# Reordering the start of a transformer block's forward and backward kernel, with two deviations by ScalarE's root and some stores on another queue

## The chip, the cores and the metric

One core of one Trainium2 chip runs the whole kernel as one program. The metric is the device time of one execution in microseconds (us); several executions are timed and the median is given. The engines are PE (TensorE; PEld is its weight load), DVE (VectorE), ACT (ScalarE), POOL (GpSimd) and SP (SyncE, which here only issues transfers). SP, ACT and POOL can each issue DMAs into a queue of their own. Every engine executes its own list of instructions in order, and waits for other engines through semaphores.

## The reference

A pre-LN transformer block, forward and then the gradients of all inputs and weights, in bfloat16, for 2048 rows of width 512, 32 heads of 16, a hidden width of 1792 and a window of 8 positions with a stride of 2:

```python
qkv = (layernorm(x) @ wqkv)            # 32 heads of 16
idx = pos[:, None] - arange(8) * 2     # each row looks at 8 earlier rows
logits = einsum("bhsd,bhswd->bhsw", q, k[idx]) * 16 ** -0.5   # -1e9 where idx < 0
h  = x + einsum("bhsw,bhswd->bhsd", softmax(logits), v[idx]) @ wo
h2 = h + gelu(layernorm(h) @ w1 + b1) @ w2 + b2
# outputs: h2, and by jax.vjp of h2 with grad_out:
# gradients of x, wqkv, wo, w1, b1, w2, b2
```

The outputs that the text below names are out_1, the gradient of x ("gx"), and out_2, the gradient of wqkv (its pieces are "wgsq").

## The kernel before, in words

The 2048 rows are worked in four chunks (0 to 3) of 512 rows, each of four tiles of 128. For each chunk the forward attention comes first (norm, projections k, q, v, products, softmax, output projection), then the feed-forward part, then the backward pass; the weight gradients and the gradient of x of the last chunk end the program.

**How the order is set.** The functions of the kernel do not issue instructions; they record operations in a `Plan` (lines 62 to 145), each with its engine, its estimated cost, and what it reads and writes. `emit` (L118) then issues them in the order of a long table of numbers, `ORDER` (from L1283), and a second table, `HOMES` (from L1367), gives every buffer its place in SBUF or its bank in PSUM. So on each engine the operations stand in a fixed list, and an operation whose input is late holds up all that stand behind it on that engine. Two tensors that have the same PSUM banks in HOMES follow each other: the later one is written only when the earlier has been read out. On SP, eight semaphores are used in rotation for its DMAs, so the ninth transfer waits for the first to land.

**The names around the change.** `load` (L267) fetches inputs and `store` (L271) writes results, both on SP unless told otherwise. `evict` (L280) copies a PSUM tensor to SBUF on ACT (L283). The first norm (`layernorm`, L338) of chunk 0 goes tile by tile: tiles 1 and 3 (`STA`) get their sums on ACT (L348 to L351), tiles 0 and 2 on DVE (L368, L369), then a root on ACT (L375), a reciprocal (L378) and the scaling (L395) on DVE. PE transposes the result (L434) and three copies on ACT and one on DVE put it into `ln1T` of chunk 0.

For chunks 1 to 3 the four tiles are done together: sums on DVE (L368 and L369, four times), variance plus epsilon on DVE (`ve`, L380), the power -1/2 on POOL (L383), mean times the reciprocal deviation on DVE (L386), then four scalings on ACT (L391, x as input and `ln1_1` for chunk 1 as output). The transposed `ln1T` of these chunks comes by a DMA transpose on SP (L277).

`p1_proj` (L648) makes k and q for the chunk with `ln1T`: 16 matmuls on PE each (L658), in two halves of two PSUM banks, and evicts each half into `kt0` or `qt0` on ACT. `p1_v` (L668) makes v (L683, evicted to `tmv`). `dots` (L502) forms the products of q with the shifted k on DVE (`prf`, L506) and sums them over a head on PE (L514). `p1_attn` (L714) does the softmax: mask (L720), maximum (L723), its subtraction by a matmul with minus the identity (`nident`, made on ACT in L320; L728), exponent on ACT (L731). ACT keeps one table of functions at a time; L310 and L312 are one-column roots and exponents that bring a table in early. The second half of the forward pass starts with L810; the feed-forward work needs `ln2T`.

At the end, `ln_bwd` (L582) takes the input gradient of the norm from PSUM (matmuls of `p3_gl1`, L1030): ACT scales and sums (L588, L590), DVE sums the product with the norm's output (L591), ACT forms `u` (L594), and DVE adds (L600, L601) to give `gx`, of which `p3_gl1` stores four pieces of a chunk (L1038). Each piece reads all four tiles. The last matmuls are groups of `wg_group` (L1042) that sum the gradient of wqkv (L1056); each group is cast on ACT (L283) and stored from SP (L273). The setting `GXP` (L1269) lists which pieces of `gx` are stored by POOL's queue.

Of the kernel before, what the change touches and what calls it, by code (L numbers as in the profile page):

```python
# [13 lines left out]
ACT = mybir.ActivationFunctionType  # L14
ALU = mybir.AluOpType
# [6 lines left out]
EPS = 1e-5  # L22
# [126 lines left out]
def kernel(  # L149
# [21 lines left out]
    V, A, T, G, SY = nc.vector, nc.scalar, nc.tensor, nc.gpsimd, nc.sync  # L171
# [4 lines left out]
    S, D = xf.shape  # L176
# [8 lines left out]
    scale = DH ** -0.5  # L185
# [14 lines left out]
    mhalf = cst("mhalf", [P, TPC], F32)  # L200
# [70 lines left out]
    def store(dst, ap, src, src_ap, kb, key=None, skey=None, q="SP", tag="store", row=1):  # L271
        e, us = (SY, 0.45) if q == "SP" else (G, 0.6)
# [65 lines left out]
    def layernorm(c, src, MV, ST, VE, NM, R, mv, st, ve, nm, rs, dst, eng, tag, per=TPC):  # L338
        sk = lambda j: None if tag == "1" and c in PM else j
        for g0 in range(0, TPC, per):  # L340
# [38 lines left out]
            else:  # L379
                op("DVE", 0.08, lambda s=s, sq=sq: V.tensor_scalar(out=ve[:, s], in0=mv[:, s, 1], scalar1=1.0 / D if sq else EPS, scalar2=EPS if sq else None, op0=ALU.mult if sq else ALU.add,  # L380
                                                                   **({"op1": ALU.add} if sq else {})),
                   r=[(MV, t) for t in ts], w=[(VE, k)], tag="ve" + tag)
                op("POOL", 1.1, lambda s=s: G.tensor_tensor(out=rs[:, s], in0=ve[:, s], in1=mhalf[:, 0:per], op=ALU.pow), r=[(VE, k), MHALF],  # L383
                   w=[(R, t) for t in ts], tag="pow" + tag)
# [620 lines left out]
    def p3_gl1(c):  # L1005
# [31 lines left out]
        for j, ap in enumerate(perm_rows(gxf[c * CH:(c + 1) * CH, :])):  # L1037
            store(None, lambda ap=ap: ap, gx, lambda j=j: gx()[32 * j:32 * j + 32], 128, q="POOL" if (c, j) in GXP else "SP", tag="gxst")  # L1038

# [128 lines left out]
    for i in range(0 if W2PE else 4):  # L1168
        r = F // 4
# [93 lines left out]
STA = (1, 3)  # L1263
WQA = ()
# [4 lines left out]
GXP = ((2, 0), (2, 1), (2, 2), (2, 3), (3, 0), (3, 1), (3, 2), (3, 3))  # L1269
# [165 lines left out]
```

## Time and profile before

| what | value |
|---|---|
| median of 3 runs | 548.23 us (546.52 to 549.38) |
| the profiled execution | 548.3 us |
| its span | 546.4 us |
| mean granted clock of PE | 0.99 |
| PE busy | 529.8 us (97%) |
| DVE busy | 467.9 us (86%) |
| ACT busy | 337.8 us (62%) |
| POOL busy | 17.5 us (3%) |

A row of the profile has the engine, the line of the kernel, the operation, the output and input tile names, shapes and the number of instructions; times are us from the start of the span. A wait's row says which engine waited at which line for what, with total, times and longest. PE's matmuls overlap its weight loads (PEld). The granted clock is the share of full speed that the chip allowed PE in that stretch.

### The profile page before, as it was taken

How to read it: one execution, taken by the hardware profiler on the slowest of the kernel's cores; microseconds unless marked ns; L12 is line 12 of the kernel's file. 1: busy time of each engine (PE TensorE's matmuls, PEld its weight loads, DVE VectorE, ACT ScalarE, POOL GpSimd, SP SyncE). 2: the span in 40 equal slices, each digit the busy share in tenths (PEclk: the TensorE clock that was granted, in tenths of full speed). 3: DMA queues.
4: the chain of work that ended last, by engine and by line, in shares of the span. 5: the costliest groups of instructions: out<-in, count | busy, mean ns of one | idle time of the engine just before them, and what ended most of it. 6: DMA issues, size and time to landing. Idle time of an engine off the chain costs nothing.

```text
span 546.4 us, 8128 instructions
## 1 busy us (share of the span) xinstructions
PE 529.8 (97%) x3063; PEld 235.4 (43%) x3063; DVE 467.9 (86%) x599; ACT 337.8 (62%) x571; POOL 17.5 (3%) x23
## 2 busy tenths in 40 slices
PE   8699989999999999999999999999999999999995
PEld 3234434444444444444444444445544444433442
DVE  4879999999999999998671329899989999999972
ACT  6848778999999967896621423224254455443763
POOL 0310000200000100000000000000000000000003
PEclk9979999999999999999999999999999999999998
DMA  7997899999998999999999999899999899999977
GB/s 192 208 278 242 222 296 290 234 259 286 228 246 264 288 248 187 251 279 197 237 165 208 197 212 216 193 298 226 247 333 302 299 310 267 276 308 299 284 218 214
DMA packets 236247, 136.62 MB, mean 250 GB/s; under 512 B 188400, under 2 KB 229552, under 8 KB 232112
## 3 DMA queue, kind: packets, MB, share of 16 engines
q1 hardware_dynamic: 235824, 135.06, 97.4%
q0 software_dynamic: 384, 1.05, 0.7%
q8 instruction: 24, 0.39, 0.3%
q14 instruction: 15, 0.12, 0.1%
HBM read 54.73 MB, written 37.84 MB: 169 GB/s over the span
## 4 chain that ended last, share of the span: by engine, by line
PE 87%; DMA 6%; ACT 2%; DVE 1%; SPq 1%; issue 1%; POOL 0%; POOLq 0%; DVEq 0%; ACTq 0%
PE ps L1056 27%; PE ps L864 9%; PE ps L892 9%; PE ps L906 9%; PE ps L810 8%; PE ps L1030 8%; PE ps L554 6%; PE ps L658 3%; PE ps L930 3%; PE ps L514 2%; PE ps L774 2%; DMA w<-in_B_w_dram 2%; DMA ln2T<-ln 1%; DMA ln1T<-ln 1%; PE ps L683 1%; DMA wk<-in_A_wqkv_dram 1%
## 5 line engine op out<-in xcount | busy, mean ns | idle before, releaser
L892 PE MATMUL ps<-goT,w2T 128*128 128x512 bf16 x224 | 52.5, 379 | 0.0
L864 PE MATMUL ps<-w,gl 128*128 128x512 bf16 x224 | 51.6, 379 | 0.2 <-DMA w<-in_B_w_dram 0.2
L906 PE MATMUL ps<-w1T,xb 128*128 128x512 bf16 x224 | 51.6, 379 | 0.0
L810 PE MATMUL ps<-ln2T,w 128*128 128x512 bf16 x224 | 50.3, 379 | 0.8 <-DMA ln2T<-ln 0.8
L1030 PE MATMUL ps<-wqkvT,gqkvT 128*128 128x512 bf16 x192 | 44.1, 379 | 0.3 <-ACT gvs L559 0.3
L283 ACT CAST wgs<-ps 128x512 bf16<-128x512 f32 (+1 forms) x30 | 15.8, 561 | 45.3 <-PE ps L1056 45.2
L812 ACT ACTIVATE xb<-ps,b1c 128x512 bf16<-128x512 f32 x56 | 35.1, 689 | 10.8 <-PE ps L810 10.7
L894 DVE SCALAR_TENSOR_TENSOR xb<-xb,ps 128x512 bf16<-128x512 bf16 x56 | 36.7, 681 | 5.4 <-PE ps L892 4.9
L1056 PE MATMUL ps<-gw1in,ln 128*128 128x512 bf16 (+1 forms) x192 | 39.3, 353 | 0.0
L1056 PE MATMUL ps<-gor,gw2in 128*128 128x512 bf16 x168 | 39.2, 379 | 0.0
L545 DVE TENSOR_TENSOR prbq<-Rq,cfq 128x4096 bf16<-128x4096 bf16 x16 | 36.0, 2286 | 1.4 <-PE ps L554 1.1
L545 DVE TENSOR_TENSOR prbv<-Rv,cfv 128x4096 bf16<-128x4096 bf16 x16 | 35.9, 2284 | 0.7 <-DMA Rv<-go_d 0.7
L545 DVE TENSOR_TENSOR prbo<-Ro,cfo 128x4096 bf16<-128x4096 bf16 x16 | 36.0, 2285 | 0.2
L506 DVE TENSOR_TENSOR prf<-qt,kt 128x4096 bf16<-128x4096 bf16 x16 | 36.0, 2279 | 0.0
L506 DVE TENSOR_TENSOR prb<-got,vw 128x4096 bf16<-128x4096 bf16 x16 | 35.8, 2284 | 0.2
L545 DVE TENSOR_TENSOR prbk<-Rk,cfk 128x4096 bf16<-128x4096 bf16 x16 | 35.8, 2282 | 0.0
L1056 PEld LDWEIGHTS <-ln 128*128 128x128 bf16 x256 | 24.6, 98 | 24.0 <-issue 1.9
L810 PEld LDWEIGHTS <-w 128*128 128x128 bf16 x224 | 21.5, 98 | 28.0 <-issue 3.1
L864 PEld LDWEIGHTS <-gl 128*128 128x128 bf16 x224 | 21.7, 98 | 27.3 <-issue 1.3
L892 PEld LDWEIGHTS <-w2T 128*128 128x128 bf16 x224 | 21.9, 98 | 26.6 <-issue 0.4
L906 PEld LDWEIGHTS <-xb 128*128 128x128 bf16 x224 | 21.9, 98 | 26.5
L588 ACT ACTIVATE gyr<-ps,rstd 128x512 bf16<-128x512 f32 x28 | 19.0, 680 | 19.0 <-PE ps L1030 12.8
(162 smaller groups left out, 924.8 us busy)
## 6 DMA issues: line engine op xcount, KB each, us to landing
Ro<-v_d SPq DMA_DIRECT2D x4, 1280.0 KB, 7.1
Rq<-k_d SPq DMA_DIRECT2D x4, 1280.0 KB, 7.0
Rv<-go_d SPq DMA_DIRECT2D x4, 1280.0 KB, 5.7
Rk<-q_d SPq DMA_DIRECT2D x4, 1280.0 KB, 7.4
g_d<-gl SPq DMA_DIRECT2D x9, 512.0 KB, 4.0
gh_d<-xb SPq DMA_DIRECT2D x9, 512.0 KB, 4.1
Ro<-v_d SPq DMA_DIRECT2D x4, 1024.0 KB, 6.8
Rq<-k_d SPq DMA_DIRECT2D x4, 1024.0 KB, 8.1
```

Source lines behind the costliest of these rows:

```text
L506: op("DVE", tt_us(4096), lambda g=g, pr=pr: V.tensor_tensor(out=pr(), in0=ql()[:, g, :].unsqueeze(1).to_broadcast([P, W, 512]), in1=_sub(k ...
L545: V.tensor_tensor(out=pr().rearrange("p a j (d h) -> p a j d h", h=H), in0=_sub(R()[:, o0, 0:1], [[st, 2], [512, 4], [32, DH], [1, H]]), i ...
L554: T.matmul(ps()[32 * j:32 * j + 32, :], lhsT=S4[:], rhs=pr()[:, hf, j, :], start=(hf == 0), stop=(hf == 1), skip_group_check=True)
L588: op("ACT", act_us(D, 1, True), lambda: A.activation(out=gyr()[:, j, :], in_=ps(), func=ACT.Copy, scale=rs[:, t:t + 1], accum_out=sg_[:, i ...
L810: T.matmul(ps(), lhsT=w1()[:, dc, f * P:(f + 1) * P], rhs=cols(ln2T[c], dc, c in FM2), start=(dc == 0), stop=(dc == DC - 1))
L812: op("ACT", act_us(512, 1), lambda f=f, ps=ps, xb=xb, f0=f0: A.activation(out=xb()[:, f - f0, :], in_=ps(), func=ACT.Identity, bias=b1c[:, ...
L864: T.matmul(ps(), lhsT=d["g"][f // 4]()[:, f % 4, j * P:(j + 1) * P], rhs=w2()[:, f, :], start=(f == 0), stop=(f == FT - 1))
L892: T.matmul(ps(), lhsT=w2T()[:, dc, f * P:(f + 1) * P], rhs=cols(goT, dc, True), start=(dc == 0), stop=(dc == DC - 1))
L894: op("DVE", 0.61, lambda f=f, ps=ps, z=z, f0=f0: V.scalar_tensor_tensor(out=z()[:, f - f0, :], in0=z()[:, f - f0, :], scalar=1.0, in1=ps() ...
L906: T.matmul(ps(), lhsT=d["d"][f // 4]()[:, f % 4, j * P:(j + 1) * P], rhs=w1T()[:, f, :], start=(f == 0), stop=(f == FT - 1))
L1030: T.matmul(ps(), lhsT=gT()[:, j, b * P:(b + 1) * P], rhs=wqkvT()[:, k0 + b, :], start=(i == 0 and b == 0), stop=(i == 2 and b == 3))
L1056: T.matmul(ps()[:, 0:N], lhsT=l, rhs=r, start=(n == 0), stop=(n == k - 1))
```

## The change

Four things are different. First, the tables ORDER and HOMES are replaced by others: the first loads and chunk 1's norm are placed by hand. Second, for chunks 1 and 2 (`RSA`) the deviation of the first norm is a root on ACT, directly from the variance, and a reciprocal on DVE, in place of the addition on DVE and the power on POOL. Third, `store` gets a third queue, ACT's own. Fourth, of the `gx` pieces that POOL stored (those of chunks 2 and 3) chunk 2's go to SP and chunk 3's to ACT's queue. No operation of PE is added or taken away. The table shows one line, since its numbers name nothing:

```diff
     def store(dst, ap, src, src_ap, kb, key=None, skey=None, q="SP", tag="store", row=1):
-        e, us = (SY, 0.45) if q == "SP" else (G, 0.6)
+        e, us = (SY, 0.45) if q == "SP" else (A, 0.5) if q == "ACT" else (G, 0.6)
...
             else:
-                op("DVE", 0.08, lambda s=s, sq=sq: V.tensor_scalar(out=ve[:, s], in0=mv[:, s, 1], ...
-                   r=[(MV, t) for t in ts], w=[(VE, k)], tag="ve" + tag)
-                op("POOL", 1.1, lambda s=s: G.tensor_tensor(out=rs[:, s], in0=ve[:, s], in1=mhalf[:, 0:per], op=ALU.pow), ...
+                if tag == "1" and c in RSA:
+                    op("ACT", 0.25, lambda s=s, sq=sq: A.activation(out=ve[:, s], in_=mv[:, s, 1], func=ACT.Sqrt, bias=epsc[:], scale=...),
+                       r=[(MV, t) for t in ts] + [EPSC], w=[(VE, k)], tag="sd" + tag, mode=7)
+                    op("DVE", 0.1, lambda s=s: V.reciprocal(out=rs[:, s], in_=ve[:, s]), r=[(VE, k)], w=[(R, t) for t in ts], tag="rc" + tag)
+                else:
+                    ...
...
-            store(None, lambda ap=ap: ap, gx, ..., 128, q="POOL" if (c, j) in GXP else "SP", tag="gxst")
+            store(None, lambda ap=ap: ap, gx, ..., 128, q="ACT" if (c, j) in GXP else "SP", tag="gxst")
...
+RSA = (1, 2)
...
-GXP = ((2, 0), (2, 1), (2, 2), (2, 3), (3, 0), (3, 1), (3, 2), (3, 3))
+GXP = tuple((3, j) for j in range(4))
...
 ORDER = (
-    7, 63, 64, 0, 10, 8, 65, 66, 4, 6, 42, 5, 26, 25, 3, 21, 24, 27, 22, 9, 30, 33, 28, 31,
+    0, 7, 5, 4, 42, 6, 25, 26, 27, 24, 21, 22, 30, 31, 28, 29, 23, 32, 34, 35, 33, 1, 2, 3,
```

In the changed kernel the lines behind these edits stand 5 or 6 lower (L391 is L396, L594 is L599, L731 is L736); L381 and L383 are the new root and reciprocal.

Start of the program on SP, before, from its first instruction on (xt0 to xt3 are the chunks' x, a 128x512 or 32x4x512 piece has 128 KB; wk, wq, wv are the thirds of wqkv, 512 KB each):

```order
L268 DMA xt0_0_1_96<-in_A_x_dram 128x512 x3
L268 DMA b1b<-in_B_b1_dram 14x128
L268 DMA xt0_0_1_96<-in_A_x_dram 128x512
L268 DMA xt1_12_3_114<-in_A_x_dram 32x4x512 x2
L268 DMA wk_15_4_121<-in_A_wqkv_dram 128x4x512
L268 DMA xt1_12_3_114<-in_A_x_dram 32x4x512 x2
L268 DMA wq_18_5_125<-in_A_wqkv_dram 128x4x512
L268 DMA xt2_20_6_128<-in_A_x_dram 32x4x512
L268 DMA xt3_21_7_130<-in_A_x_dram 32x4x512
L268 DMA xt2_20_6_128<-in_A_x_dram 32x4x512 x3
L268 DMA wv_25_8_135<-in_A_wqkv_dram 128x4x512
```

The same place on SP, after:

```order
L268 DMA xt0_1_2_98<-in_A_x_dram 128x512 x3
L268 DMA b1b<-in_B_b1_dram 14x128
L268 DMA xt0_1_2_98<-in_A_x_dram 128x512
L268 DMA xt1_6_3_104<-in_A_x_dram 32x4x512 x4
L268 DMA wk_10_4_109<-in_A_wqkv_dram 128x4x512
L268 DMA wq_11_5_111<-in_A_wqkv_dram 128x4x512
L268 DMA xt2_12_6_113<-in_A_x_dram 32x4x512 x4
L268 DMA wv_16_7_118<-in_A_wqkv_dram 128x4x512
```

All four pieces of chunk 1's x now stand ahead of wk, chunk 2's x stands together behind wq, and the first piece of chunk 3's x no longer stands ahead of wv. Further down the transposing DMA of chunk 1 (L277) stands behind the four zero stores and two small stores of k and q; wo, two pieces of x and one of grad_out, which stood ahead of it, now stand behind it.

ACT at the start, before, from the eviction of chunk 0's ln1T on (kt0 and qt0 are k and q of chunk 0, tmv its v, e the exponents of the softmax):

```order
L283 COPY ln1T0_62_15_204<-ps 128x4x128 x3
L283 CAST kt0_39_11_167<-ps 128x2x512 x2
L283 CAST qt0_91_14_266<-ps 128x1024
L391 ACTIVATE ln1_1_92_14_268<-xt1_12_3_114,rstd1 128x512 x4
L283 CAST qt0_91_14_266<-ps 128x1024
L283 CAST tmv_116_19_332<-ps 128x1024
L283 CAST tmv_120_21_342<-ps 128x1024
L391 ACTIVATE ln1_2_124_18_354<-xt2_20_6_128,rstd1 128x512 x4
L312 ACT_TABLE_LOAD
L312 ACTIVATE tb0<-epsc 128x1
L731 ACTIVATE e_138_18_385<-ps 128x1024
```

The same place on ACT, after (ve1 is the root; the first L381 is chunk 1's, the second chunk 2's):

```order
L283 COPY ln1T0_55_13_191<-ps 128x4x128 x3
L381 ACTIVATE ve1<-mv1,epsc 128x4
L320 ACTIVATE nident<-ident 128x128
L283 CAST kt0_75_10_231<-ps 128x2x512
L312 ACT_TABLE_LOAD
L312 ACTIVATE tb0<-epsc 128x1
L381 ACT_TABLE_LOAD
L381 ACTIVATE ve1<-mv1,epsc 128x4
L283 CAST kt0_75_10_231<-ps 128x2x512
L283 CAST qt0_88_10_258<-ps 128x1024
L396 ACTIVATE ln1_1_90_11_262<-xt1_6_3_104,rstd1 128x512 x4
L283 CAST qt0_88_10_258<-ps 128x1024
```

Both roots, nident's copy (which stood ahead of the ln1T copies), the early exponent and a table load back to the root now stand ahead of chunk 1's four scalings, and the second cast of kt0 stands behind chunk 2's root.

The end of ACT's list, before (gyr1, c0 and u1 are steps of `ln_bwd`):

```order
L590 ACTIVATE c0<-sg 128x1
L594 ACTIVATE u1_1958_16_4991<-ln1b_1699_41_4298,c0,sx 128x512
L283 CAST wgsq_1971_11_5006<-ps 128x512 x2
L283 CAST wgsq_1976_7_5012<-ps 128x512 x2
```

And after, where the gx in question is that of chunk 3:

```order
L599 ACTIVATE u1_1953_18_4981<-ln1b_1612_40_4015,c0,sx 128x512 x2
L599 ACTIVATE u1_1936_23_4948<-ln1b_1612_40_4015,c0,sx 128x512
L273 DMA out_1_dram<-gx_1963_16_4997 128x1x512 x3
L283 CAST wgsq_1974_6_5015<-ps 128x512 x2
L283 CAST wgsq_1976_5_5018<-ps 128x512
L273 DMA out_1_dram<-gx_1963_16_4997 128x1x512
L283 CAST wgsq_1976_5_5018<-ps 128x512
```

Three of the four stores of gx stand ahead of the last four casts and one between the last two; before, POOL's list held them.

More of the change, by code (lines that the diff above doesn't have):

```diff
@@ L379, in layernorm @@
             else:
-                op("DVE", 0.08, lambda s=s, sq=sq: V.tensor_scalar(out=ve[:, s], in0=mv[:, s, 1], scalar1=1.0 / D if sq else EPS, scalar2=EPS if sq else None, op0=ALU.mult if sq else ALU.add,
-                                                                   **({"op1": ALU.add} if sq else {})),
-                   r=[(MV, t) for t in ts], w=[(VE, k)], tag="ve" + tag)
-                op("POOL", 1.1, lambda s=s: G.tensor_tensor(out=rs[:, s], in0=ve[:, s], in1=mhalf[:, 0:per], op=ALU.pow), r=[(VE, k), MHALF],
-                   w=[(R, t) for t in ts], tag="pow" + tag)
+                if tag == "1" and c in RSA:
+                    op("ACT", 0.25, lambda s=s, sq=sq: A.activation(out=ve[:, s], in_=mv[:, s, 1], func=ACT.Sqrt, bias=epsc[:], scale=1.0 / D if sq else 1.0),
+                       r=[(MV, t) for t in ts] + [EPSC], w=[(VE, k)], tag="sd" + tag, mode=7)
+                    op("DVE", 0.1, lambda s=s: V.reciprocal(out=rs[:, s], in_=ve[:, s]), r=[(VE, k)], w=[(R, t) for t in ts], tag="rc" + tag)
+                else:
+                    op("DVE", 0.08, lambda s=s, sq=sq: V.tensor_scalar(out=ve[:, s], in0=mv[:, s, 1], scalar1=1.0 / D if sq else EPS, scalar2=EPS if sq else None, op0=ALU.mult if sq else ALU.add,
+                                                                       **({"op1": ALU.add} if sq else {})),
+                       r=[(MV, t) for t in ts], w=[(VE, k)], tag="ve" + tag)
+                    op("POOL", 1.1, lambda s=s: G.tensor_tensor(out=rs[:, s], in0=ve[:, s], in1=mhalf[:, 0:per], op=ALU.pow), r=[(VE, k), MHALF],
+                       w=[(R, t) for t in ts], tag="pow" + tag)
             if "ACT" in [eng[j] for j in js] or (tag == "1" and LX):
@@ L1037, in p3_gl1 @@
         for j, ap in enumerate(perm_rows(gxf[c * CH:(c + 1) * CH, :])):
-            store(None, lambda ap=ap: ap, gx, lambda j=j: gx()[32 * j:32 * j + 32], 128, q="POOL" if (c, j) in GXP else "SP", tag="gxst")
+            store(None, lambda ap=ap: ap, gx, lambda j=j: gx()[32 * j:32 * j + 32], 128, q="ACT" if (c, j) in GXP else "SP", tag="gxst")
     PAIR = []
```

236 rows, old and new, of tables (HOMES, ORDER) are left out of this document.

## The prediction

> **What bounds the kernel now.** I read the page first, then PE's waits, then windows, then the timeline of both ends. On the page the line of engines gives each one's busy time, and the chain's line says who set the end.
>
> ```profile
> PE 529.8 (97%) x3063; PEld 235.4 (43%) x3063; DVE 467.9 (86%) x599; ACT 337.8 (62%) x571; POOL 17.5 (3%) x23
> ...
> PE 87%; DMA 6%; ACT 2%; DVE 1%; SPq 1%; issue 1%; POOL 0%; POOLq 0%; DVEq 0%; ACTq 0%
> ```
>
> PE works 529.8 of 546.4 us. The change takes no matmul away, so it can win only from PE's waits, from its clock and from the two ends. The waits (who waits, for whom, total, times, longest):
>
> ```profile
> PE ps L658 <- DMA ln1T<-ln: 2.4, 1, 2.4
> PE ps L514 <- DVE prf L506: 1.7, 1, 1.7
> ...
> PE ps L810 <- DMA ln2T<-ln: 0.8, 1, 0.8
> PE ps L683 <- DMA wv<-in_A_wqkv_dram: 0.7, 1, 0.7
> PE ps L728 <- DVE mx L723: 0.7, 1, 0.7
> PE ps L554 <- ACT gks L559: 0.7, 1, 0.7
> ```
>
> These six make 7.0 us, 4.8 of them before 28 us. The windows (length, busy time of PE, PEld, DVE, ACT, POOL, granted clock, DMA share, GB/s) place the rest:
>
> ```profile
> 22.93:26.36 3.43, 0.62 (x8) 0.23 (x8) 3.43 (x4) 2.70 (x5) 0.14 (x1) 1.00 1.00 192
> 26.36:33.19 6.83, 5.66 (x25) 1.60 (x25) 3.67 (x5) 2.72 (x4) 0.00 (x0) 0.50 0.84 211
> 36.70:75.00 38.30, 38.30 (x267) 17.85 (x265) 37.88 (x37) 30.21 (x46) 2.49 (x2) 1.00 0.86 260
> 75.00:78.00 3.00, 1.52 (x7) 0.46 (x6) 3.00 (x3) 1.95 (x2) 0.00 (x0) 1.00 1.11 236
> 99.00:490.00 391.00, 391.00 (x2213) 175.71 (x2215) 338.06 (x437) 233.45 (x395) 5.36 (x3) 1.00 1.02 249
> 490.00:500.00 10.00, 9.03 (x71) 3.14 (x60) 10.00 (x5) 4.06 (x7) 0.00 (x0) 1.00 1.12 321
> ```
>
> Three things are to be seen. PE never pauses from 99 to 490. Its clock is halved from 26.36 to 33.19, so 5.66 us of work there would be 2.83 at full clock: 2.8 us lost. From 36.7 to 75 DVE is busy 37.88 of 38.30, so nothing there can slip on DVE without PE soon feeling it. The late windows leave PE idle 1.48 (75 to 78) and 0.97 us (490 to 500).
>
> **The change part by part: the start.** This is the timeline (start, duration) of the first 30 us:
>
> ```profile
> 7.41 0.28 ACT L375 ACTIVATE ve<-mv,epsc 128x1 f32<-128x1 f32 x1
> ...
> 7.71 0.17 DVE L378 RECIPROCAL rstd<-ve 128x1 f32<-128x1 f32 x1 [0.63 <-ACT ve L375]
> ...
> 8.86 0.29 ACT L320 ACTIVATE nident<-ident 128x128 bf16<-128x128 bf16 x1
> ...
> 10.48 3.38 PEld L658 LDWEIGHTS <-wk 128*128 128x128 bf16 x16 [0.60 <-DMA wk<-in_A_wqkv_dram]
> 10.72 3.61 PE L658 MATMUL ps<-ln1T,wk 128*128 128x512 bf16 x16 [0.67 <-ACT ln1T L283]
> ...
> 11.52 0.69 DVE L368 BATCH_NORM_STATS2 st<-xt 128x6 f32<-128x512 bf16 x1 [1.52 <-DMA xt<-in_A_x_dram]
> ...
> 13.51 1.93 ACT L283 CAST kt<-ps 128x1024 bf16<-128x1024 f32 x2 [2.84 <-PE ps L658]
> ...
> 14.63 0.18 DVE L369 BATCH_NORM_AGGREGATE mv<-st 128x2 f32<-128x6 f32 x1
> ...
> 15.10 1.04 POOL L383 TENSOR_TENSOR rstd<-ve,mhalf 128x4 f32<-128x4 f32 x1 [13.65 <-DVE rstd L386]
> ...
> 16.44 0.69 DVE L368 BATCH_NORM_STATS2 st<-xt 128x6 f32<-128x512 bf16 x1 [1.36 <-DMA xt<-in_A_x_dram]
> ...
> 18.06 0.13 DVE L386 SCALAR_TENSOR_TENSOR rstd<-mv,rstd 128x4 f32<-128x4 f32 x1
> ...
> 18.22 2.93 ACT L391 ACTIVATE ln<-xt,rstd 128x512 bf16<-128x512 bf16 x4 [1.11 <-DMA wv<-in_A_wqkv_dram]
> ...
> 18.54 3.63 PE L683 MATMUL ps<-wv,ln1T 128*128 128x512 bf16 x16 [0.75 <-DMA wv<-in_A_wqkv_dram]
> ...
> 19.92 2.28 DVE L506 TENSOR_TENSOR prf<-qt,kt 128x4096 bf16<-128x4096 bf16 x1
> ...
> 21.18 2.98 SPq L277 DMA_TRANSPOSE ln1T<-ln  x1
> ...
> 27.53 3.57 PE L658 MATMUL ps<-ln1T,wk 128*128 128x512 bf16 x8 [2.37 <-DMA ln1T<-ln]
> 27.61 1.28 ACT L312 ACT_TABLE_LOAD   x1
> ...
> 28.91 0.20 ACT L312 ACTIVATE tb<-epsc 128x1 f32<-128x1 f32 x1
> ```
>
> Loads land in the order of their bytes. The 1536 KB of chunk 0, chunk 1 and wk are in at 11.5 and the 2688 KB that end with chunk 2's last piece at 16.44: 1152 KB in 4.9 us, 234 KB/us. Now wk stands behind all of chunk 1, 256 KB deeper, 1.1 us later: 10.48 becomes about 11.5, and k starts 0.8 late. Chunk 0's last root also stands behind both of ACT's sums now, so its transpose is ready at about 11.5 too; the two delays lie beside each other. wv is 128 KB earlier, 18.1, and its 0.7 wait is swallowed by what follows.
>
> DVE reaches chunk 1's sums after its own copy of ln1T at about 11.5, as before, and ends them 3.3 later (14.63+0.18), at 14.8. The root costs 0.28, the reciprocal 0.17, the scaling 0.13: ready at 15.4. Before, ve and the POOL power took until 16.14, and the scaling then stood behind two of chunk 2's sums until 18.06. So the deviation itself comes 2.8 us earlier. What ACT does with it is another matter, since its queue now holds, in order: that root (to 15.1), the 128x128 nident copy (0.29, to 15.4), one kt cast (0.97, to 16.4), a table load and one exp (1.28+0.20), a load back to the root (1.28; 19.2), chunk 2's root. The latter needs chunk 2's sums: x in at 2560 KB, 15.9, plus 3.3, 19.2 to 19.3; it ends at 19.6. Load and sums therefore cover each other; without that cover either costs its 2.8 alone. Then kt's second cast and qt's first, 0.97 each, to 21.5, and only now the four norms of chunk 1, 2.93, to 24.4. Before, they ran from 18.22 to 21.15: 3.2 us later, the opposite of what the earlier deviation suggests.
>
> Who waits for it: q's first half uses the PSUM banks of k's first half, so PE waits for the kt cast until 16.4 (k ended at 15.1, 1.3 idle). v's second half uses those of qt and waits for 21.5 (0.8). v ends at 24.1 instead of 22.17. The first product prf starts at 21.5 instead of 19.92. Chunk 1's transpose:
>
> ```profile
> DMA to landing us min/median/max: 4.2/4.9/6.3
> ```
>
> It was 27.49 less 21.18, the slow end 6.3, with six transfers (wo, xp, gor, zeros) ahead of it; now these stand behind it. From 24.4 it lands at 28.6 by the fast end and 30.7 by the slow. I take 28.6, since the queue is empty ahead of it: PE starts chunk 1's k at 28.6 for 27.53, +1.1, bounds +0.6 (a transpose a little under the fastest row) and +3.2. The halved clock I keep at its 2.8: PE still has a gap of some 4 us there, so it adds nothing to the sum, and -2.8 is a bound.
>
> On the load itself the Trainium skill speaks against the change: its page "ScalarE: Activation LUTs", section "What ACT_TABLE_LOAD costs", gives every switch of set a drain of about 1.38 us beside the load. Here the row behind the 1.28 load starts 0.02 after its end (27.61+1.28, 28.91), so the trace shows no such drain, and I count none.
>
> **The middle.** Work per engine is the same; both tables keep nearly the same neighbours, though most positions differ by a few. I take 0, bounds -2.45 (the idle time of both late windows gone) and +4.6 (two prf-sized products of 2.28 late in the stretch where DVE is full).
>
> **The end.** Rows of the last 10 us and of the stores (KB, median us to landing), and what ended last on SP:
>
> ```profile
> 536.72 2.97 PE L1056 MATMUL ps<-gks,ln1b 128*128 128x512 bf16 x13
> ...
> 537.56 0.69 DVE L601 TENSOR_TENSOR gx<-u,gyr 128x1024 bf16<-128x1024 bf16 x1
> ...
> 538.55 2.15 POOL L273 DMA_DIRECT2D out_dram<-gx  x4 [1.04 <-DVE gx L601]
> 539.73 0.58 ACT L283 CAST wgsq<-ps 128x512 bf16<-128x512 f32 x1 [1.14 <-PE ps L1056]
> ```
>
> ```profile
> out_dram<-gx SPq DMA_DIRECT2D x8, 128.0 KB, 2.8
> ...
> out_dram<-gx POOLq DMA_DIRECT2D x8, 128.0 KB, 4.6
> ```
>
> Call E the end of the matmuls, 539.69. Before, the last gx store is issued at E+1.0 and lands 4.6 later or a little less, about E+5.1, and the last wgsq eviction ends at E+0.6. Afterwards eight matmul groups instead of nine (0.86 each) follow the last input gradient, so gx is done at E-0.9 (E-1.4 before). ACT then issues three stores (0.54 each by POOL's row, plus 0.3 until the first starts) until E+1.0, casts three times (0.58) until E+2.8, issues the fourth (E+3.3) and casts the last wgsq by E+3.9. SP's last store then lands 2.8 later at its 256 KB, taken as SP's gx row: about E+6.3 with some overlap of the issues, E+6.7 without: +1.2; if an issue holds ACT for nothing, wgsq is done at E+0.6 again and gx lands at E-0.6+4.6: -0.9; if the last store takes 4.6, +3. The four stores that move from POOL to SP add some 2.2 us of issues there (0.54 each); behind them on SP stand only the two last wgsq stores, whose casts come after E, so I cost them at nothing. If gx of that chunk came late, the first wgsq store would slip, not the last.
>
> **Sum.** 548.3 + 1.1 + 0 + 1.2 = 550.6 against the profiled execution, whose 548.3 stands at the median of the runs (548.23): 550.5 us, +0.41%. A measurement of this kernel tells about 0.5%, 2.74 us, from no change.
>
> **The rivals.** A is the forecast, chance 0.45, own range 546.8 (tail -0.9, start +0.6, late waits half gone) to 553.8 (start +3.2, tail +2.3); two thirds of it inside 0.5%, 0.30 same and 0.15 slower.
>
> B, slower: the order between 36.7 and 75 puts two DVE products ahead of the softmax steps that PE waits for. For it: DVE has only 0.42 us of slack in 38.3 and starts 1.6 us later with prf; against it: the neighbours in the table are nearly the same. Each costs 2.28, from the point at which the slip passes PE's lead: 550.5 + 4.6 = 555.1. Chance 0.17.
>
> C, faster: the gap at 23 us becomes too short for the halved clock (-2.8), and the new order also closes both late windows (-2.45): 550.5 - 5.25 = 545.3, and 543.2 if ACT's issues cost nothing besides; middle 544.3. For it: the gap shrinks by about 1 us as v ends later, and the waits there are single ones. Against it: three things must agree. Chance 0.23.
>
> D, no difference: the halved clock alone goes, 550.5 - 2.8 = 547.7. The window of 3.43 us with 0.62 of work is what precedes the fall at 26.36. Chance 0.12, of which 0.02 faster. The Trainium skill, "TensorE: Matmul & The Clock Gate", section "What's actually happening", gives a free-running window of about 3.4 us, whose whole idleness halves the clock. By that rule the gap's place decides, not its length alone; the trace's 3.43 us agrees.
>
> F, slower: ACT pays after each of the two added loads what the trace does not show, up to one more load's length each (1.28), so chunk 1's norms come 2.6 later: 553.1. Chance 0.03; by the skill's drain it would be 1.38 each.
>
> **How the numbers follow.** Faster 0.23 + 0.02 = 0.25; same 0.30 + 0.10 = 0.40; slower 0.15 + 0.17 + 0.03 = 0.35. The range goes from C's middle, 544.3, to just over B, 555.5, which leaves out half of C and about half of B. Likeliest is A, so 550.5; A's own range stands above.
>
> **What would show it.** Right: ACT's second root near 19.6 behind a second table load; PE waiting for a kt cast near 16; chunk 1's norms from 21 on and its ln1T landing past 28; clock 0.5 for some 7 us after it; at the end three ACT issues of half a microsecond ahead of three casts, and the last wgsq store over 3 us after the last matmul. Wrong: norms of chunk 1 before 19 (a root that waits for nobody), k of chunk 1 at 27.5 or sooner, a clock that never falls, new waits for DVE products between 36 and 78, or wgsq casts that run at E+0.6.

## The result, and the profile after

The changed kernel takes 551.96 us (median of 4 runs, 551.27 to 552.02) against 547.57 (4 runs, 546.52 to 549.38): the ratio on record is 1.0104, with a 95% interval of 1.0076 to 1.0132 (the quotient of these two medians is 1.0080, near the interval's lower end). It is slower by 4 to 7 us. The profiled execution took 551.27 us with a span of 549.5, 3.1 more than the one shown of before.

The page of the changed kernel, engines and chain:

```profile
PE 530.6 (97%) x3063; PEld 234.8 (43%) x3063; DVE 469.6 (85%) x599; ACT 340.5 (62%) x575; POOL 9.6 (2%) x13
...
PE 82%; DMA 5%; DVE 3%; ACT 1%; ACTq 0%; issue 0%; DVEq 0%; SPq 0%
```

PE has as much to do as before; it waits more. Its waits:

```profile
PE ps L663 <- DMA ln1T<-ln: 2.1, 1, 2.1
PE ps L519 <- DVE prf L511: 1.7, 1, 1.7
...
PE ps L688 <- ACT qt L283: 1.1, 1, 1.1
PE ps L663 <- ACT kt L283: 0.9, 1, 0.9
PE ps L815 <- DMA ln2T<-ln: 0.9, 1, 0.9
PE ps L869 <- DMA w<-in_B_w_dram: 0.8, 1, 0.8
PE ps L741 <- ACT e L736: 0.8, 1, 0.8
```

The wait for wv is gone, as forecast. Two waits for ACT's casts (0.9 and 1.1) have come, and three that the forecast did not have: 0.8 for w2 at the first L869 matmul and 0.8 for the exponents (0.2 each before), and 0.4 for a product of DVE at 51.93:

```profile
51.93 0.61 PE L559 MATMUL ps<-prbo,S 128*32 128x512 bf16 x8 [0.41 <-DVE prbo L550]
```

That is one of the prediction's signs of being wrong, a new wait for a DVE product between 36 and 78. `prbo` is the product of the softmax's result with the gathered v. In return before's wait of 0.7 for DVE's maximum (L728, at 76 us) is gone. The start, from the timeline:

```profile
10.96 3.62 PE L663 MATMUL ps<-ln1T,wk 128*128 128x512 bf16 x16 [0.61 <-ACT ln1T L283]
...
14.04 0.30 ACT L381 ACTIVATE ve<-mv,epsc 128x4 f32<-128x4 f32 x1 [3.18 <-DVE mv L369]
...
15.46 1.28 ACT L312 ACT_TABLE_LOAD   x1
...
15.59 0.69 DVE L368 BATCH_NORM_STATS2 st<-xt 128x6 f32<-128x512 bf16 x1 [0.71 <-DMA xt<-in_A_x_dram]
...
16.75 0.20 ACT L312 ACTIVATE tb<-epsc 128x1 f32<-128x1 f32 x1
...
16.96 1.28 ACT L381 ACT_TABLE_LOAD   x1
...
18.91 0.30 ACT L381 ACTIVATE ve<-mv,epsc 128x4 f32<-128x4 f32 x1 [0.67 <-DVE mv L369]
...
19.12 0.99 ACT L283 CAST kt<-ps 128x1024 bf16<-128x1024 f32 x1
...
20.01 1.01 ACT L283 CAST qt<-ps 128x1024 bf16<-128x1024 f32 x1
...
20.92 2.93 ACT L396 ACTIVATE ln<-xt,rstd 128x512 bf16<-128x512 bf16 x4
...
21.06 2.29 DVE L511 TENSOR_TENSOR prf<-qt,kt 128x4096 bf16<-128x4096 bf16 x1 [2.18 <-ACT qt L283]
```

The queue on ACT is as forecast: the second root waits for DVE's sums until 18.91, the two casts, the norms and the first product stand behind it. Chunk 1's k starts at 28.74 for 27.53 (forecast 28.6).

A load of the exponent's table that the order's first rows did not show stands further down, ahead of the softmax's exponents:

```profile
35.91 1.28 ACT L736 ACT_TABLE_LOAD   x1 [2.52 <-DVE mx L728]
...
38.28 0.61 PE L741 MATMUL ps<-e,ident 128*128 128x128 bf16 x8 [0.82 <-ACT e L736]
```

The early exponent brought its table in at 15.46, the second root threw it out at 16.96, and the third load comes where PE waits for the exponents. Last, the stores at the end, where the last matmul ends at 542.25:

```profile
537.47 7.49 SPq L273 DMA_DIRECT2D out_dram<-gx  x7
...
540.51 1.99 ACTq L273 DMA_DIRECT2D out_dram<-gx  x3
542.54 0.59 ACT L283 CAST wgsq<-ps 128x512 bf16<-128x512 f32 x1 [3.99 <-PE ps L1061]
542.61 0.58 ACTq L273 DMA_DIRECT2D out_dram<-gx  x1
543.02 1.57 ACT L283 CAST wgsq<-ps 128x512 bf16<-128x512 f32 x3
545.05 1.08 SPq L273 DMA_DIRECT2D out_dram<-wgsq  x2
```

ACT's first three issues take 0.66 each and hold the casts until 542.54; the fourth runs beside a cast. The last wgsq store leaves at 545.70, 3.45 after the last matmul (0.65 before). But the casts are done at 544.6; SP comes later because three gx stores stand ahead of its last two. The first of these three left only at 543.09, 2.4 us after SP's issue before it, and SP's own waits say for what:

```profile
SPq L273 <- DMA out_dram<-gx: 2.3, 1, 2.3
```

SP waited for another gx store to land. ACT's first, issued at 540.51, would land at 543.1 by the median of its queue (2.5), so I take it that ACT and SP share the eight semaphores; no run tests that by itself.

### The profile page after: what moved, and what is told of

It is laid out like the page before. It is cut to its first block, busy times and chain, and to the rows that moved or that the text cites. A ratio compares the mean times of both kernels' runs of the same rounds, so it can differ in the third digit from the quotient of the medians.

```text
span 549.5 us, 8150 instructions
## 1 busy us (share of the span) xinstructions
PE 530.6 (97%) x3063; PEld 234.8 (43%) x3063; DVE 469.6 (85%) x599; ACT 340.5 (62%) x575; POOL 9.6 (2%) x13
## 4 chain that ended last, share of the span: by engine, by line
PE 82%; DMA 5%; DVE 3%; ACT 1%; ACTq 0%; issue 0%; DVEq 0%; SPq 0%
PE ps L1061 26%; PE ps L869 9%; PE ps L911 9%; PE ps L897 9%; PE ps L815 8%; PE ps L1035 6%; PE ps L559 5%; PE ps L935 3%; PE ps L779 2%; PE ps L519 2%; DVE prbo L550 2%; DMA w<-in_B_w_dram 2%; PE ps L663 1%; DMA ln2T<-ln 1%; DMA gqkvT<-gks 1%; DMA Rv<-go_d 1%
## 5 line engine op out<-in xcount | busy, mean ns | idle before, releaser
L869 PE MATMUL ps<-w,gl 128*128 128x512 bf16 x224 | 52.0, 379 | 0.8 <-DMA w<-in_B_w_dram 0.8
L1061 PE MATMUL ps<-gw1in,ln 128*128 128x512 bf16 (+1 forms) x192 | 38.8, 353 | 0.0
L839 ACT ACTIVATE xb<-xb 128x2048 bf16<-128x2048 bf16 (+1 forms) x16 | 26.8, 1690 | 12.0 <-DVE xb L838 12.0
L815 PEld LDWEIGHTS <-w 128*128 128x128 bf16 x224 | 21.4, 98 | 28.6 <-issue 3.7
L869 PEld LDWEIGHTS <-gl 128*128 128x128 bf16 x224 | 21.7, 98 | 27.2 <-DMA w<-in_B_w_dram 1.3
```

The lines of the kernel that those rows point to most:

```text
L815: T.matmul(ps(), lhsT=w1()[:, dc, f * P:(f + 1) * P], rhs=cols(ln2T[c], dc, c in FM2), start=(dc == 0), stop=(dc == DC - 1))
L839: op("ACT", act_us(N), lambda xb=xb: A.activation(out=fl(xb), in_=fl(xb), func=ACT.Tanh, scale=GC), w=[xb], tag="tanh", mode=6)
L869: T.matmul(ps(), lhsT=d["g"][f // 4]()[:, f % 4, j * P:(j + 1) * P], rhs=w2()[:, f, :], start=(f == 0), stop=(f == FT - 1))
L1061: T.matmul(ps()[:, 0:N], lhsT=l, rhs=r, start=(n == 0), stop=(n == k - 1))
```

## The experiments

Every kernel was compared with the kernel before in the same session. The ratios are those on record; the quotients of the medians differ from them by up to 0.0024 (a_root2_tail 1.0028, b_wait 1.0016) and lie inside the intervals. Two ratios whose intervals overlap are not told apart by them. `_after(ORDER, ((i, j), ...))` takes operation i out of the table and puts it directly behind operation j. 12 kernels ran, in three groups.

| run | what it is | ratio to before | 95% interval |
|---|---|---|---|
| (the change) | | 1.0104 | 1.0076 to 1.0132 |
| a_pow2 | change, chunk 2's deviation by POOL | 1.0082 | 1.0054 to 1.0110 |
| a_exp_late | change, tables loaded as before | 1.0105 | 1.0080 to 1.0129 |
| a_root2_late | a_exp_late, chunk 2's root behind chunk 1's norms | 1.0059 | 1.0040 to 1.0079 |
| a_gx_pool | change, chunk 3's gx on POOL | 1.0124 | 1.0091 to 1.0156 |
| a_root2_tail | a_root2_late, all gx stores as before | 1.0040 | 1.0022 to 1.0058 |
| a_w2 | a_root2_tail, w2's load earlier | 1.0160 | 1.0130 to 1.0191 |
| b_gx | before, gx stores as in the change | 1.0026 | 1.0006 to 1.0046 |
| b_root_nm | before, roots on ACT | 1.0008 | 0.9989 to 1.0027 |
| b_wait | before, chunk 2's root ahead of two casts | 1.0030 | 1.0008 to 1.0053 |
| b_prod2 | before, one DVE product twice | 1.0034 | 1.0015 to 1.0054 |
| b_sums | before, two sums earlier on PE | 0.9985 | 0.9969 to 1.0000 |
| b_sums_root | b_sums and b_root_nm | 0.9984 | 0.9961 to 1.0008 |

**First group: ACT's list at the start, and the tail.** The theory was the forecast's own: ACT's list at the start and the added table loads set most of the loss. The rival was that the new order as a whole sets it.

a_pow2:

```diff
-RSA = (1, 2)
+RSA = (1,)
```

> The changed kernel with chunk 2's deviation given back to DVE's addition and POOL's power (RSA holds chunk 1 alone); chunk 1 keeps the root. Theory 1, ACT's list at the start and the two added table loads set most of the loss: without chunk 2's root ACT needs no load back to the root, kt's second cast comes at 17 instead of 19.1, chunk 1's norms at 19 instead of 20.9, its ln1T about 1.9 earlier, and the exponent before the softmax finds its table (0.6 more): about 549, 0.3 to 0.5% above the kernel before. Theory 2, the new order as a whole sets it and an earlier start is lost again at the next wait: 551 to 552, 0.8% above or more.

Measured 1.0082. The norms started at 18.92 and the first product at 19.06, as theory 1 said, and there was no further table load until 81.8. But theory 1 had 1.003 to 1.005, and the ratio is at theory 2's 0.8%: of at least 0.5% that was expected to go, 0.2% went, and the interval overlaps that of the change. In its profile DVE then waited 1.4 for a gather that had not landed, and PE waited 1.9 at 93 for oT, the transposed attention output that the matmuls with wo read: part of the earlier start was lost again, as the rival has it.

a_exp_late:

```diff
+ORDER = _after(ORDER, ((12, 289),))
```

(12 is the early exponent, 289 the last of chunk 2's norms.)

> The changed kernel with the early one-column exponent moved behind chunk 2's norms, as before has it, both roots left where they are. ACT then loads its tables as the kernel before does, once for the root and once for the exponent. Theory 1: chunk 2's root still waits for its sums until 18.9 and kt's second cast stands behind it, so chunk 1's norms stay at 20.9 and its ln1T at 28.7; only the load before the softmax goes, 0.6: about 550.9. If the table loads themselves were the start's loss, the norms would come 2 us earlier and the time would fall to 549. Theory 2: 551 to 552.

Measured 1.0105: nothing. The two added loads are gone, the load ahead of the softmax too (PE's wait for the exponents, 0.8 in the changed kernel, is back at before's 0.2), and the norms still start at 21.09. So the table loads are not the loss at the start. The wait of the root for its sums covers them, as the forecast said.

a_root2_late:

```diff
+ORDER = _after(ORDER, ((12, 289), (286, 183), (287, 109), (288, 287)))
```

(286 is chunk 2's root, 183 the last of chunk 1's norms, 287 and 288 its reciprocal and scaling, 109 the second product.)

> The kernel of the second run with chunk 2's root moved behind chunk 1's four norms as well, and its reciprocal and scaling behind the second product on DVE. Theory 1: kt's two casts run back to back to 16.4, qt's first cast follows q's first half to 18.3, the norms start at 18.3 instead of 20.9, ln1T lands at about 26.2, and the softmax finds its table: 2.5 and 0.6 less, about 548.5. Theory 2: 551 to 552, with the gain lost at the waits for DVE products or weights after 37.

Measured 1.0059, 0.45% under a_exp_late beside it, or 2.5 us: only the places of the root and of its reciprocal and scaling have changed. Its ACT list:

```profile
14.44 0.99 ACT L283 CAST kt<-ps 128x1024 bf16<-128x1024 f32 x1
...
16.13 1.01 ACT L283 CAST kt<-ps 128x1024 bf16<-128x1024 f32 x1 [0.70 <-PE ps L663]
17.86 1.01 ACT L283 CAST qt<-ps 128x1024 bf16<-128x1024 f32 x1 [0.71 <-PE ps L663]
18.77 2.93 ACT L396 ACTIVATE ln<-xt,rstd 128x512 bf16<-128x512 bf16 x4
18.91 2.29 DVE L511 TENSOR_TENSOR prf<-qt,kt 128x4096 bf16<-128x4096 bf16 x1 [0.70 <-ACT qt L283]
```

The casts now wait for PE, not for chunk 2's sums, and the first product starts 2.1 earlier than in the changed kernel.

a_gx_pool:

```diff
-            store(None, lambda ap=ap: ap, gx, ..., 128, q="ACT" if (c, j) in GXP else "SP", tag="gxst")
+            store(None, lambda ap=ap: ap, gx, ..., 128, q="POOL" if (c, j) in GXP else "SP", tag="gxst")
```

> The changed kernel with the last chunk's four gx stores on POOL's queue, as before, the others left on SP. Theory 1: ACT casts wgsq as its matmuls end, SP no longer waits for a semaphore that an ACT store holds, and the last wgsq store leaves about 0.7 after the last matmul instead of 3.5; POOL's transfers land up to 5 after their issue, so the time from the last matmul to the end goes from 7.3 to 6.6 and the whole to about 550.8. Rival: the order of stores on SP alone sets the end, and nothing moves: 551.5.

Measured 1.0124, whose interval overlaps the changed kernel's; the runs spread from 550.6 to 555.39, and the profiled one is the slowest. Its tail is 7.34 (553.6 less 546.26), no shorter: POOL could not start before 545.17, when a transfer of SP's had landed, and its stores land last. SP still had chunk 2's gx stores ahead of wgsq. So one half of the store change alone settles nothing. What the profile does show is the start: chunk 2's x came late, its sums began at 17.39, the second root followed at 20.73, and the first product at 22.87. With the root ahead of the casts, whatever delays chunk 2's x delays chunk 1.

**Second group: who sets the time, and single parts in the old order.** The windows from the first product to the first L864 matmul (before) or L869 (after), with the columns of the prediction's windows, suggested another theory, the third. First before, then the changed kernel:

```profile
19.92:98.31 78.39, 72.38 (x481) 31.23 (x480) 74.71 (x73) 59.48 (x84) 5.47 (x3) 0.96 0.89 259
```

```profile
21.06:100.48 79.42, 72.73 (x483) 31.50 (x482) 74.84 (x70) 62.06 (x85) 2.56 (x2) 0.96 0.91 267
```

DVE is busy for 74.7 of 78.4 us, more than PE (72.4). In the stretch from 20 to 98, what counts is when DVE gets its first product, and what it waits for after. PE is full only behind that.

b_gx has the store line and GXP of the change in the old order:

```diff
-GXP = ((2, 0), (2, 1), (2, 2), (2, 3), (3, 0), (3, 1), (3, 2), (3, 3))
+GXP = tuple((3, j) for j in range(4))
```

> The kernel before in its old order, with only the stores of gx changed: the last chunk's four on ACT's queue, the chunk's before on SP. Three of them stand ahead of two wgsq casts on ACT, the fourth between the casts. Theory 1, the stores on ACT hold up the casts and, through the semaphores that ACT and SP share, SP's last stores: the tail from the last matmul to the end grows from 6.7 to about 7.3, so about 0.5 slower, 546.5 against 546. Rival, the tail of the changed kernel comes from its order (eight groups of matmuls behind the last gradient in place of nine) and not from the queue: 546, or 0.5 faster, since these transfers land sooner than POOL's.

Measured 1.0026. Its profile's tail (last matmul to the end) against before's 6.71:

```profile
536.84:545.30 8.46, 0.00 (x1) 0.00 (x0) 0.00 (x0) 2.05 (x4) 0.00 (x0) 0.77 0.78 232
```

The stores alone cost 1.4 us by the ratio. In its profile three issues on ACT end at 537.42 and hold the casts, and SP's gx stores run until 538.51 with wgs, wgso and wgsq stores behind them. Here the order is before's, so the choice of queues alone does it.

b_root_nm has the branch on RSA of the change, and this:

```diff
+RSA = (1, 2)
...
+ORDER = _after(ORDER, ((181, 180),))
```

(181 is chunk 1's scaling, 180 its reciprocal.)

> The kernel before in its old order, with the roots of chunks 1 and 2 on ACT and one move: chunk 1's scaling directly behind its reciprocal on DVE. No table load is added, since the early exponent still stands behind chunk 2's norms. Theory 1, what hurts in the changed kernel is what stands on ACT ahead of the norms, not the root: chunk 1's norms start at about 17.2 instead of 18.2, its ln1T and PE's k come 1 us earlier, the first product stays at 19.9 behind chunk 2's sums; the wait of the mask on DVE shrinks by up to 1: 545.0 to 546.0, ratio 0.998 to 1.000. If the root itself were the loss: 1.003 or more.

Measured 1.0008, no difference: the root is not the loss. That the expected gain stayed out too may be because it was worked out from before's profile, which shows a late start. Its k of chunk 1 came at 27.53, but b_gx and b_prod2, which have the same program up to there, have it at 26.45 and 26.19; b_root_nm has 25.96.

b_sums:

```diff
+ORDER = _after(ORDER, ((192, 112), (191, 114)))
```

(112 and 114 are the sums of the third and fourth product, 192 and 191 two k groups of chunk 1.)

> The kernel before with two moves on PE only: the sums of chunk 0's third product go ahead of chunk 1's first k matmuls and those of the fourth between the two groups of k. DVE's mask then need not wait 3.1 for them. Theory 3, formed on the runs so far: from the first product (19.9) to the first L864 matmul (98.3) DVE is busy 74.7 of 78.4 us and sets the time, so what DVE is spared there comes off the end: the mask 2.5 earlier, the first L864 matmul 2 to 2.5 earlier, ratio 0.996. Theory 1, PE's own waits set the time: the order of k and sums on PE changes only where it waits, at most 0.6 of sums moved into its gap: ratio 0.999 to 1.000.

Measured 0.9985, 0.8 us less instead of 2.2. In its profile the mask still waits 2.1 and the reciprocal of the softmax 1.2, and from the first product to the first L864 matmul it takes 77.3. Most of the wait moved. The interval just reaches 1, so nothing was won that is clear of noise, and theory 3 got little more than a third of its gain. Chunk 1's k starts at 28.25 here, for 26.45 and 26.19 in b_gx and b_prod2, and nothing was lost by that either.

b_prod2 does one product twice into the same place:

```diff
-            op("DVE", tt_us(4096), lambda g=g, pr=pr: V.tensor_tensor(
+            op("DVE", tt_us(4096), lambda g=g, pr=pr, n=2 if (pl.stage, g, tag) == (3, 2, "f") else 1: [V.tensor_tensor(
...
-                in1=..., op=ALU.mult),
+                in1=..., op=ALU.mult) for _ in range(n)],
```

> The kernel before with one product of 2.28 us on DVE done twice (chunk 2, third group, at 54.5 us), the second time over the first; nothing else changes. Theory 3, DVE sets the time from 20 to 98 us: the first L864 matmul is 2.0 to 2.3 later and so is the end, ratio 1.004. Theory 1, PE sets it and DVE has a lead there: PE's waits grow by less than 1, ratio 1.000 to 1.002.

Measured 1.0034, 1.9 us for 2.28 us of work on an engine with 86% of the span (the interval's lower end, 1.0015, still lies inside theory 1's 1.002). PE's new waits end at 57.4 and 64.8 us, 1.2 and 0.8. From the first product to the first L864 matmul it takes 79.0, and b_gx, the same program up to the doubled product, 76.3. So DVE does set the time there, and the earlier theory, that PE's own waits do, falls for this stretch.

**Third group: the cause put into the old order, and what is left.** When chunk 2's x arrives differs from run to run, so the step from the first of chunk 2's sums to the first product is what compares the kernels (starts in us, from the timelines):

| kernel | first of chunk 2's sums | first product | between |
|---|---|---|---|
| before | 16.44 | 19.92 | 3.48 |
| b_prod2 | 14.73 | 18.21 | 3.48 |
| the change | 15.59 | 21.06 | 5.47 |
| a_gx_pool | 17.39 | 22.87 | 5.48 |
| a_root2_late | 14.91 | 18.91 | 4.00 |
| b_wait | 15.12 | 20.66 | 5.54 |

Before, the product follows the sums on DVE at once (3.48 is four sums). With the root ahead of two casts it comes 2.0 later: the root's 0.3 and the casts' 0.99 and 1.01 less their overlaps.

b_wait is b_root_nm's branch with ACT's list changed so:

```diff
+ORDER = _after(ORDER, ((84, 286), (87, 84), (185, 87), (184, 185), (182, 184), (183, 182)))
```

(84 is kt's second cast, 87 qt's first, 182 to 185 chunk 1's norms.)

> The kernel before in its old order, with both roots on ACT and one thing of the new order put in: chunk 2's root stands ahead of kt's second cast, and so of qt's first cast and chunk 1's norms, on ACT. No table load is added and the stores are the old ones. Theory 3, the loss at the start is that two casts of about 1 us and the root stand behind chunk 2's sums, and DVE, which sets the time from the first product on, gets that product 5.5 after the first of chunk 2's sums instead of 3.5: 2.0 to 2.3 later, ratio 1.004 to 1.005 (the root alone measured 1.0008). Theory 1, the table loads and the softmax's exponent are the loss: ratio 1.001 to 1.002.

Measured 1.0030. The step is there, 5.54, and so is a cost, clear of before, but smaller: 1.2 us above b_root_nm, not 2, and the two intervals overlap. From the first product to the first L869 matmul this kernel takes 75.9, less than before's 78.4, and DVE's mask waits 1.5 instead of 3.1: the later first product takes away part of a wait for PE that came after it. Theory 1's 1.001 to 1.002 lies inside the interval, so the ratio alone does not decide; the step does, with a_exp_late (no gain from the table loads) and a_root2_late (2.5 us from the root's place, its interval apart from a_exp_late's).

a_root2_tail has a_root2_late's table, "POOL" in the store line and before's GXP.

> The kernel of run a_root2_late with the stores of gx as before, chunk 2's and chunk 3's on POOL's queue, so that SP's last wgsq store has no gx store ahead of it and ACT none among its casts. If ACT's and SP's gx stores cost 1.2 at the end: tail from the last matmul 6.2 instead of 7.4, ratio 1.004 instead of 1.0059. If the order (eight groups of matmuls behind the last gradient) sets the tail: 7.3 as in a_gx_pool, ratio 1.006.

Measured 1.0040, 1.0 us below a_root2_late; the two intervals overlap, so it is the profile that shows the tail:

```profile
541.91:548.00 6.09, 0.00 (x1) 0.00 (x0) 0.00 (x0) 0.58 (x1) 0.96 (x2) 0.92 0.54 160
```

That is what the six other kernels with before's stores have too (5.98 to 6.29); a_root2_late has 7.42, and before's own 6.71 is the odd one. What is left is 1.0040, or 2.2 us. The first product stands at 19.04, no later than before's, but from there to the first L869 matmul it takes 80.1, and the old order 75.9 to 78.4 (79.0 with the doubled product). So what is left lies at least in part in the new order between 19 and 99 us; some of it may still be the start's, since the step from chunk 2's sums (14.78) to the first product is 4.26 here for 3.48 before. Its PE waits from 85 to 103:

```profile
PE ps L869 <- DMA w<-in_B_w_dram: 1.2, 1, 1.2
PE ps L779 <- DMA oT<-ost: 1.0, 1, 1.0
```

Those two waits stand in the new order's profiles in changing shares (w2 0.8 to 1.5 in all six, oT 0.7 to 1.9 in four); before had 0.2 for w2 and none for oT. They are not the only candidates. An earlier one stands on DVE, the engine that sets this stretch: it waits for the gather of chunk 0's v (`Ro`) ahead of its products with the softmax's result. First here, then in b_gx:

```profile
DVE prbo L550 <- DMA Ro<-v_d: 3.3, 1, 3.3
```

```profile
35.73 0.59 SPq L501 DMA_DIRECT2D Ro<-v_d  x1
40.97 2.29 DVE L550 TENSOR_TENSOR prbo<-Ro,cfo 128x4096 bf16<-128x4096 bf16 x1 [3.27 <-DMA Ro<-v_d]
```

```profile
31.94 0.67 SPq L496 DMA_DIRECT2D Ro<-v_d  x1
38.82 2.29 DVE L545 TENSOR_TENSOR prbo<-Ro,cfo 128x4096 bf16<-128x4096 bf16 x1
```

Of the five old-order profiles whose first product comes at much the same time (18.2 to 19.3), four start this product at 38.5 to 38.8 and b_sums at 40.2, and no old-order profile has the wait. In the new order the gather leaves later, since wo and pieces of x and grad_out, which stood ahead of chunk 1's transposition, now stand among v's stores, ahead of the gathers. The 2.2 us between the two rows are as much as is left, but no run moved those transfers. In the changed kernel the wait is hidden: DVE gets to this product only at 42.98.

a_w2 tries to take the first away:

```diff
+ORDER = _after(ORDER, ((12, 289), (286, 183), (287, 109), (288, 287), (491, 236)))
```

(491 is w2's load, 236 the gather ahead of the transposition.)

> The kernel of run a_root2_tail with one move on SP: the load of w2 ahead of chunk 2's transposing DMA of oT, behind the last gather. In the five runs of the new order so far PE waited 0.8 to 1.5 for this load at its first L869 matmul (0.2 in before). If the load's place sets that: the wait gone, the first L869 matmul 1 earlier, ratio 0.002 below the run beside it. If the transfer only trades places with the transposition, the wait for oT grows by the same and nothing is won.

Measured 1.0160, 6.6 us worse. SP's queue there:

```profile
85.22 0.39 SPq L268 DMA_DIRECT2D w<-in_B_w_dram  x1
86.39 10.20 SPq L277 DMA_TRANSPOSE oT<-ost  x1
...
98.66 0.61 PE L779 MATMUL ps<-wo,oT 128*128 128x512 bf16 x1 [7.12 <-DMA oT<-ost]
```

Behind the 1792 KB load the issue of the transposition took 10.20 us instead of 4.09 (a_root2_tail) or 2.76 (changed kernel) and PE waited 7.1 for it. They did trade places, at a worse price than expected. How the last 2.2 us split among these waits stays open, since no kernel took one away alone.

b_sums_root, the two parts of the old order together:

```diff
+RSA = (1, 2)
...
+ORDER = _after(ORDER, ((181, 180), (192, 112), (191, 114)))
```

> The kernel before with the parts that did no harm or helped: both roots on ACT and chunk 1's scaling behind its reciprocal, and on PE the sums of the third and fourth product ahead of and between chunk 1's k matmuls; the stores and the rest of the order as before. Both theories: k of chunk 1 comes a little earlier, DVE's mask waits less: ratio 0.996 to 0.999, the fastest of all.

Measured 0.9984, interval 0.9961 to 1.0008: not clear of before, and no better than b_sums. It beats the changed kernel by 1.2%.

## Why the prediction was right, and where not

**Direction and the queue on ACT: right; the size short.** The forecast was 550.5, 0.4% slower; measured 551.96, 1.0% slower. With 0.5% as the least that can be told from no change, the prediction gave "same" the larger chance (0.40, slower 0.35), and it is slower. That the two times lie so near is in part luck: the sum started from a before of 548.3, and its medians in the three later sessions were 546.0 to 547.0, so the terms forecast add up to 2.3 us and those measured to some 5.7. At the start it rested on ACT's order, and the rows bear it out one by one: second root at 18.91 (forecast 19.6), norms at 20.92 (21.5), k of chunk 1 at 28.74 (28.6), the root waiting for nobody but its sums, the added table loads hidden (a_exp_late: 1.0105 for 1.0104). PE's wait for kt's cast ended at 15.49 (forecast 16.4), since DVE began chunk 1's sums at 10.73, not at 11.5, and so the root that stands ahead of the cast came at 14.04.

**The size of the start: less than half.** The sum took +1.1, through ln1T and PE. a_root2_late is worth 2.5 us against a_exp_late. Two things were wrong. First, one profiled execution was taken for before's start, and it was a late one (26.19 and 26.45 in the other profiles with the same start). Second, the path named was not the one that carries: the first product, which the prediction dated 1.6 later without using it in the sum, is what DVE waits for, and DVE sets most of the next 75 us (b_prod2), while a later k of chunk 1 cost b_sums nothing. The window at 36.7 with DVE busy 37.88 of 38.30 said so, and I used it only for rival B.

**"I take 0" for the middle: this is the step that failed.** The sum put the new order there at nothing because the neighbours in the tables looked nearly the same; 2.2 us are left when start and tail are put back (a_root2_tail, 1.0040). The bound of +4.6 held it. The mechanism of B, products ahead of the softmax's steps, is not what was found, though its sign, a new wait of PE for a DVE product, came with 0.4 us. What the profiles show in its place are waits for transfers on SP's queue: DVE's for v's gather at 41 us, and PE's for w2's load and the oT transposition at 90 to 100. The prediction saw that wo, x and grad_out no longer stand ahead of chunk 1's transposition, and counted the gain; that they now hold up v's gather it did not ask. Which of these waits makes the 2.2 us was not shown. The wait for a table load ahead of the exponents was missed as well, because I read ACT's order only as far as chunk 1's norms; taking it away won nothing (a_exp_late).

**The tail: size right, mechanism half.** +1.2 forecast; a_root2_tail against a_root2_late gives 1.0 by the ratio and 1.3 by the profiles' tails, b_gx alone 1.4. ACT's three issues do stand ahead of the casts (0.66 each for 0.54). That SP's last stores wait for a semaphore that ACT holds, and for chunk 2's gx stores, which I costed at nothing, was not foreseen; it is read from the profile and only the two together were taken away.

**The rivals.** The clock: D did not occur in the changed kernel's profile; the granted clock was 0.5 from 27.65 to 34.48:

```profile
27.65:34.48 6.83, 5.74 (x25) 1.66 (x26) 3.83 (x5) 2.75 (x4) 0.00 (x0) 0.50 0.92 274
```

In other runs it lasted half as long. In a_gx_pool it was

```profile
31.10:34.52 3.42, 3.42 (x15) 1.04 (x17) 2.00 (x3) 0.72 (x2) 0.00 (x0) 0.50 1.06 326
```

and so had b_prod2, b_root_nm and b_sums (3.41). Whether the halving takes one such window or two differs among profiles whose programs agree up to there (before two, b_gx and b_prod2 one). The Trainium skill, "TensorE: Matmul & The Clock Gate", section "What's actually happening", gives a free-running window of about 3.4 us; these stretches of 3.41 and 6.83 agree with one and two of them. The prediction's "whole idleness" does not come out of its own row: PE worked 0.62 us in the 3.43 before the fall.

The prediction also priced the halving at 2.8 us by PE's work alone. a_root2_late and a_root2_tail are one program as far as the gx stores; after 25 us the one profile has a halved clock for 3.4 us and the other has none. The stretches from the first product to the first L869 matmul, first a_root2_late:

```profile
18.91:98.70 79.79, 72.88 (x483) 31.85 (x488) 75.42 (x74) 63.84 (x91) 2.57 (x2) 0.98 0.94 267
```

```profile
19.04:99.11 80.07, 71.46 (x484) 31.65 (x488) 75.14 (x72) 63.98 (x91) 2.58 (x2) 1.00 0.92 265
```

Without the halving PE has 1.4 us less to do, and DVE is ready for its product with the gathered v 1.7 earlier, but the gather is not, and the stretch is no shorter. So what a halved window costs depends on what is waited for next. It is not most of a_root2_late's gain either: between a_exp_late, with two windows, and a_root2_late, with one, DVE's wait for the mask falls only from 3.0 to 2.4, while the first product comes 2.3 earlier.

F is out: behind both added loads the next activation starts within 0.01 us (15.46 + 1.28 and 16.75), or waits for DVE. The drain of about 1.38 us that the Trainium skill, "ScalarE: Activation LUTs", section "What ACT_TABLE_LOAD costs", adds to a switch is not in these rows.

## What to carry to other kernels

An operation that waits for a late input holds up all that stands behind it on its engine, so a root that is cheap by itself should not be put ahead of casts that others wait for. Ask what each engine's next wait holds up, and for every stretch which engine is full: PE was busy for 97% of the whole span and still did not set most of the first 100 us. A part of the order that "looks nearly the same" is not a reason to put its term at nothing. One profile's start is one sample: compare steps between events, not clock times, where an input's arrival varies. Stores that are moved to another queue can still hold up what ends the program, through the list of the engine that issues them and, as it seems here, through shared semaphores.

## What the runs showed of the hardware that was not expected

A transposing DMA issued behind a 1792 KB load held its queue's issuer 10.2 us and landed 12.2 us after it began (a_w2), against 2.0 to 4.1 us of issue in before, the changed kernel, a_root2_late and a_root2_tail, where it stands ahead of that load. An ACT store's issue can run beside a cast on the same engine (542.61 beside 542.54 in the changed kernel), while the cast that stands behind three issues (540.51 to 542.50) started only after the last of them. After 25 us one program showed a stretch of 3.4 us at half clock in one profile (a_root2_late) and none in another (a_root2_tail, the same up to the gx stores).
